# A gated linear recurrence with a spatial gating block on one core: all steps ordered anew, five constant products fewer

## The chip, the core and the metric

The kernel runs on one core of a Trainium2 chip. The metric is the time of one execution on the device, in microseconds. Engines are called by their names: TensorE (PE, with PEld for its weight loads), VectorE (DVE), ScalarE (ACT), GpSimd (POOL) and SyncE (SP, which only starts transfers here).

## The reference, cut to what matters

```
B, H, S, D = 4, 8, 768, 48;  d_model 384, d_ff 1024
# part 1: a recurrence with a complex decay for each of the 4 x 8 heads
a = (a_re, a_im) * min(|a|, 0.999) / (|a| + 1e-6)
for t in range(S):
    S_re, S_im = a_re*S_re - a_im*S_im + k[t] v[t]^T,  a_re*S_im + a_im*S_re
    y[t] = q[t] @ S_re
x = y with the heads side by side                       # (B, S, 384)
# part 2: a block with a gate over positions
h = gelu(x @ w_in);  u, v = halves of h
v_n = layer_norm(v) * g_ln
v_s = w_sg @ v_n + b_sg                                  # mixes the 768 positions
out = x + (u * v_s) @ w_out
```

## The kernel before

**Part 1.** The recurrence is worked in 24 chunks of 128 positions, six to each batch. Thirteen units of one or two chunks prepare them: `load` (steps `l`, `m`), `logs` (`g`: logarithms and exponentials of the gates), `scale` (`e`: the decays multiplied into `k` and `q`), `arctan` (`t`), `turns` (`p`: summed angles), `sincos` (`s`). For each chunk follow `rotate` (`r`), `heads` (`z`: features to rows; for the first batch by TensorE transposes `pk`, later through DRAM), `load_v` (`v`) and `attend` (`a`). `attend` transposes `K` (tile `pk`, copied to `kt`), makes scores `pa` in two halves, masks them into `am`, makes the state's addend `ps` and the output `py`, which takes `am` and the state `S`.

**Part 2.** `normal` (`n`) makes the v half (`pv`), Gelu and the layer norm; `expand` (`x`) makes the u half (`pu`); `spatial` (`y`) mixes positions (`pvs`), multiplies with `u` (`tg`) and makes the output products (`po`). Each operand of these is split into a high and a low part (`xh`, `xl`, `vh`, `vl`, `gh`, `gl`), and each product is made of three. The weights are split in steps `w`; `h` and `k` look at the ranges of the inputs, and `ok` (`in_range`, L858 and after) makes one flag of them which every engine reads before the last branch.

**The order.** Every step is a Python generator; a step is what it issues up to its next `yield`. The string `ORDER` (L32) names the steps one by one: `a8:2` runs two steps of chunk 8's `attend`. Each engine works its instructions in exactly that order. A quote behind a name makes a choice, by the variable `alt`: `ew` (L199) takes VectorE, or GpSimd for one quote; `evac` (L203) takes ScalarE, or VectorE for a quote; `high` (L209) takes ScalarE, GpSimd or VectorE; `low` (L218) VectorE or GpSimd. In `attend`, one quote masks by ScalarE and GpSimd (L656, L657), otherwise VectorE does it in one step (L659). `stoke` (L221) issues no, one or several constant products of 256 columns, by the quotes: they have no use in the result. Two of TensorE's instructions make one such product. `act` (L187) loads another function table whenever a step's function is of another of three sets (Ln and Exp; Arctan and Sin; Gelu).

**Narrow and wide.** Products `pa`, `ps`, `py` and `pd` take weights of at most 64 columns of the array; all others take 96 or 128.

Of the kernel before, what the change touches and what calls it, by code (L numbers as in the profile page):

```python
# [37 lines left out]
a1:2 v2 w7'' w4 w9 w4 a1:2 w12 l4 w2'' t3 s2 r2:2 p2 r3 l4 w12 g3:2 r3 g3:4 w9' w9 a1 p3 w12 m3:2 z2:2 e3 z2:5 w1'' z2
e3 w12 w8 g4:2 e3 v3 p3 e3' w12' e3 a2 a2'' a2 n0_0 a2 g4 w5 a2 w4' a2 g4:2 p3 a2'' a2 v4 a2:2 e3:2 w8'' w8' e3'' e3
e3' e3 n0_0' f z3:3 z3'' p3:2 p3'' p3 f z3:3 f:2 z3 a3:3 f:2 a3 s3:3 w12 e3 a3'' a3:4 n0_0' a3 r4'' r4 w5 w10 t4 p4 v5  # L40
w10:2' w4'' r5'' g4 n0_0:2 z4:6 n0_0:3 z4 r5'' a4 a4'' o0 z4 n0_0:2 g4 l5:2 a4:2 z5:2 w5 a4'' a4 z5' z5:2 m4 z5 g4 m4
z5:2 n0_2 w5 l7 g4 g5 w5 a5 a4:2 a4'' w11 a5' n0_2 a5 a5'' a5' w14 p4:2 e4 n0_0' n0_0'' a4 e4 o1 w11 n0_2'' n0_2 v7
# [1011 lines left out]
```

## Time and profile before

| what | before |
|---|---|
| three runs, us | 437.07, 436.69, 436.38 (median 436.69) |
| span of the profiled execution, us | 434.6 |
| median of the runs less that span, us | 2.1 |
| instructions in the profile | 10107 |
| DMA | 93.54 MB, mean 215 GB/s |

The profile is of one execution. Its span goes from the first to the last instruction; the profile gives no separate time of that execution around the span, so the difference to the median of the runs stands for it. An engine's busy time is the union of its instructions' times; TensorE's products overlap, and their ends are modelled, so that its busy share says less than the distance from one start to the next.

### The profile page before, as it was taken

The numbers are of one execution on the slowest core, as the hardware profiler recorded it, in microseconds if no ns is written. First come the engines' busy times: TensorE is split into PE (matmuls) and PEld (weight loads), VectorE is DVE, ScalarE is ACT, GpSimd is POOL, SyncE is SP. The second block draws the span as 40 slices with busy tenths as digits, with TensorE's granted clock in tenths as the row PEclk, the third lists the DMA queues.
The fourth block names the chain that finished last, engine by engine and source line by source line (L and its number), as shares of the span: only waits on it lengthen the run. The fifth ranks groups of instructions, "written<-read, shape, count | busy, mean of one in ns | idle before, by whom it ended". The sixth has DMA issues, their size and how long they took to land.

```text
span 434.6 us, 10107 instructions
## 1 busy us (share of the span) xinstructions
PE 421.3 (97%) x3958; PEld 383.6 (88%) x3958; DVE 364.5 (84%) x620; ACT 275.2 (63%) x378; POOL 150.7 (35%) x234
## 2 busy tenths in 40 slices
PE   7999899999999989999999999999999999999994
PEld 6667688788999989889998999989999998899994
DVE  5899899999999999898898999997898776757363
ACT  6999898886999886695666776776750113342010
POOL 7214356203334154446022416532321011326130
PEclk9999999999999999999999999999999999999999
DMA  7577868789478898697959789568947964554531
GB/s 244 176 205 196 268 168 278 223 241 277 149 196 259 243 299 263 208 273 212 271 141 299 217 241 252 168 193 226 320 120 230 330 193 163 187 181 166 157 116 59
DMA packets 78540, 93.54 MB, mean 215 GB/s; under 512 B 10516, under 2 KB 60438, under 8 KB 78488
## 3 DMA queue, kind: packets, MB, share of 16 engines
q1 hardware_dynamic: 78344, 92.65, 71.2%
q8 instruction: 32, 0.52, 0.5%
q10 hardware_dynamic: 144, 0.20, 0.1%
q14 instruction: 20, 0.16, 0.1%
HBM read 69.23 MB, written 23.60 MB: 214 GB/s over the span
## 4 chain that ended last, share of the span: by engine, by line
PE 43%; DVE 29%; issue 8%; POOL 7%; ACT 6%; DMA 4%; SPq 0%; DVEq 0%; POOLq 0%
PE pvs L230 10%; PE pu L230 6%; PE po L822 6%; PE pv L230 4%; PE pa L649 4%; PE py L700 2%; PE pv L225 2%; DVE am L659 2%; PE py L705 2%; DVE tg L838 2%; DVE im L510 2%; PE warm L225 2%; ACT L193 1%; PE ps L675 1%; ACT csn L194 1%
## 5 line engine op out<-in xcount | busy, mean ns | idle before, releaser
L230 PE MATMUL pvs<-wsgh,vh 128*128 128x384 f32 x192 | 65.9, 343 | 0.0
L230 PE MATMUL pvs<-wsgh,vl 128*128 128x384 f32 x192 | 65.3, 340 | 0.2
L193 ACT ACT_TABLE_LOAD x50 | 64.2, 1283 | 1.7 <-PEq L1039 0.9
L230 PE MATMUL pvs<-wsgl,vh 128*128 128x384 f32 x192 | 64.9, 338 | 0.0
L649 PE MATMUL pa<-Q,K 96*64 96x64 f32 (+1 forms) x768 | 41.0, 251 | 1.5 <-DVE am L659 1.5
L649 PEld LDWEIGHTS pa<-Q,K 96*64 96x64 f32 x768 | 36.7, 137 | 6.0 <-ACT ep L194 1.6
L700 PE MATMUL py<-am,vbuf 128*64 128x128 f32 x384 | 39.0, 276 | 2.8 <-DVE am L659 1.7
L230 PEld LDWEIGHTS pvs<-wsgh,vl 128*128 128x128 f32 x192 | 36.1, 188 | 1.4 <-DVE vl L219 0.8
L230 PEld LDWEIGHTS pvs<-wsgh,vh 128*128 128x128 f32 x192 | 36.1, 188 | 0.7 <-issue 0.4
L230 PEld LDWEIGHTS pvs<-wsgl,vh 128*128 128x128 f32 x192 | 36.1, 188 | 0.0
L822 PE MATMUL po<-gh,wouth 128*128 128x384 f32 x96 | 33.0, 344 | 0.8 <-DVE oki L873 0.8
L705 PE MATMUL py<-Q,S 96*48 96x128 f32 x320 | 33.7, 272 | 0.0
L822 PE MATMUL po<-gl,wouth 128*128 128x384 f32 x96 | 32.6, 340 | 0.3 <-DVE gl L219 0.2
L230 PE MATMUL pu<-xh,winh 128*128 128x384 f32 x96 | 32.9, 342 | 0.0
L230 PE MATMUL pu<-xh,winl 128*128 128x384 f32 x96 | 32.3, 337 | 0.0
L822 PE MATMUL po<-gh,woutl 128*128 128x384 f32 x96 | 32.3, 337 | 0.0
L230 PE MATMUL pu<-xl,winh 128*128 128x384 f32 x96 | 32.3, 336 | 0.0
L659 DVE TENSOR_TENSOR am<-pa,masks 128x512 f32<-128x512 f32 x44 | 29.5, 682 | 2.4 <-PE pa L649 2.1
L219 POOL TENSOR_TENSOR gl<-tg,gh 128x384 fp32r<-128x384 f32 x15 | 18.6, 1237 | 34.0 <-DVE gh L216 15.1
L700 PEld LDWEIGHTS py<-am,vbuf 128*64 128x64 f32 x384 | 25.5, 136 | 5.2 <-DVE am L659 3.1
L230 PE MATMUL pv<-winh,xh 128*128 128x512 f32 x72 | 29.4, 408 | 0.0
L194 ACT ACTIVATE vr<-pv 128x512 f32<-128x512 f32 x24 | 14.3, 599 | 22.7 <-PE pv L230 13.7
(286 smaller groups left out, 1125.2 us busy)
## 6 DMA issues: line engine op xcount, KB each, us to landing
vbuf<-in_t_v_dram SPq DMA_DIRECT2D x24, 288.0 KB, 3.9
K<-rk SPq DMA_DIRECT2D x18, 384.0 KB, 4.4
Q<-rq SPq DMA_DIRECT2D x18, 384.0 KB, 6.8
x<-xd SPq DMA_DIRECT2D x9, 576.0 KB, 5.6
xd<-yp SPq DMA_DIRECT2D x48, 96.0 KB, 3.5
gr<-in_f_im_dram SPq DMA_DIRECT2D x12, 384.0 KB, 5.3
gr<-in_f_re_dram SPq DMA_DIRECT2D x12, 384.0 KB, 3.9
out_dram<-x SPq DMA_DIRECT2D x23, 192.0 KB, 3.5
```

The costliest lines, as they stand in the source:

```text
L193: nc.scalar.preload_act_table_set(SETS[t])
L194: nc.scalar.activation(out, in_, func, scale=scale, **kw)
L219: ew().tensor_tensor(out=l, in0=src, in1=h.bitcast(F32), op=ALU.subtract)
L225: nc.tensor.matmul(o, mask[:, 0:n], u_turn[:, 0:o.shape[1]], start=True, stop=True, skip_group_check=True)
L230: nc.tensor.matmul(o, w(i), x(i), start=(i == 0 and j == 0), stop=(i == n - 1 and j == 2))
L510: nc.vector.tensor_tensor_scan(out=im[:, kt, :], data0=im[:, kt, :], data1=im[:, kt, :], initial=run["left", b, c0][:, kt:kt + 1] if c0 el ...
L649: nc.tensor.matmul(pa[rows, hh, j:], K(h)[:, j:j + KB], Q(h)[:, j:], start=True, stop=True)
L659: nc.vector.tensor_tensor(out=pairs(am), in0=pairs(pa), in1=causal, op=ALU.mult)
L700: nc.tensor.matmul(py[64 * e:64 * e + 64, p_, :], Vy(h)[:, 0:64], ams[h // 4][:, h % 4, :], start=True, stop=c == 0)
L705: nc.tensor.matmul(py[64 * e:64 * e + D, p_, :], Sb[:, h, :], Q(h), start=False, stop=True)
L822: nc.tensor.matmul(po[d], w[:, f, ds], g[:, f, :], start=f == 0 and j == 0, stop=f == NF - 1 and j == 2)
L838: ew().tensor_mul(tg, us[f], tg)
```

## The change

`ORDER` is replaced: 1179 names become 1457. The same steps are run, each as often; what is new is their order, and the quotes. Counted over both orders, the constant products go from 40 to 35: one ahead of `pl` of chunk 0, one each ahead of a `pk` of chunks 0, 1 and 5, and one ahead of `py` of chunk 5 go. Three generators are written so that a step reads a name later than before, and adds no instruction. The diff, with the order cut to its first and last lines:

```diff
 ORDER = """
-o0:2 l0:2 f' f:10 f' f:10 f:2' g0:5 g0' f:4 f' f:4 f' w0:4 f w0'' f t0 f' f:3 v0 w13 f' w13:3 w13'' f:3 w13' g0:2 m0:2
-f e0' w0 l1:2 g1:2 g1'' f' e0 e0'' f' f:6 f' f:2 e0 w2 p0 p0' p0 w2 s0'' g1:2 g1'' w2 s0:2 e0 w1 t1 r0'' f p0 r0 w1 l2
...
-x0_3 h5 y3_3:2' y3_3:2 y3_0 y3_0'' y3_3:6 h23 y3_0 k4 h3 y3_0' y3_0:2 x3_0 k4 h3 x3_0 y3_0'' x3_0:2 h23 y3_0:2' y3_0:2
-y3_0:2'' y3_0' y3_3 h22:2 x3_0 k5 k7:2 y3_0:2 k5 ok:2 y3_0 x3_0 y3_0:2 y3_0' y3_0'' y3_0:10
+f' f:2 l0 f:2 l0 f:2 g0 f:4 g0:2 f' f:5 g0 f w0 f g0 f:3 f:2' w0 t0 w0 f w0 f l1 f g0 w13 f v0 f' g0 w13 m0 f o0 w13
+f:2 g0 w13 f f' f:2 f' f:3 l1 f' w2 f w0'' f o0 f g1 e0' f f' g1 e0 f' w13' f g1'' e0' e0 f m0 g1 f:2 g1 f:2 f' p0 w1
...
+x3_0 k4 h17 y3_3 y3_0 h1 y3_3 y3_0'' y3_3:2 h3 y3_3 h1' y3_3:2 x3_0 h7 y3_0' y3_0 k10 f x3_0 y3_0:2 k8 x3_0:2 y3_0'
+y3_0 y3_3 y3_0 k12:2 y3_0 k8 y3_0 y3_0' y3_0'' y3_0' y3_0:4 y3_3 y3_0 y3_0' h7'' y3_0:2' y3_0 ok y3_0:7 ok y3_0
 """
@@ logs
-        re, im = (part(n, x) for x in ("re", "im"))
+        re = part(n, "re")
...
+        im = part(n, "im")
         ew().tensor_mul(im, im, e)
@@ scale
-        q_, k_ = (U[n][x] for x in ("q", "k"))
...
-            ew().tensor_mul(at(k_, i), at(k_, i), at(em, i))
+            k_ = at(U[n]["k"], i)
+            ew().tensor_mul(k_, k_, at(em, i))
...
-            ew().tensor_mul(at(q_, i), at(q_, i), at(ep, i))
+            q_ = at(U[n]["q"], i)
+            ew().tensor_mul(q_, q_, at(ep, i))
@@ attend
-        Sb = run.get(("S", g - 1))
+        Sb = lambda: run["S", g - 1]
...
-                nc.vector.tensor_tensor(out=Sn, in0=ps[0:2 * D], in1=Sb, op=ALU.add)
+                nc.vector.tensor_tensor(out=Sn, in0=ps[0:2 * D], in1=Sb(), op=ALU.add)
...
-                    nc.tensor.matmul(py[64 * e:64 * e + D, p_, :], Sb[:, h, :], Q(h),
+                    nc.tensor.matmul(py[64 * e:64 * e + D, p_, :], Sb()[:, h, :], Q(h),
```

## Rows read from the trace of the kernel before

**Rows 1.** The page's first part: busy time of each engine, its share of the span, and its instructions.
```profile
PE 421.3 (97%) x3958; PEld 383.6 (88%) x3958; DVE 364.5 (84%) x620; ACT 275.2 (63%) x378; POOL 150.7 (35%) x234
```
**Rows 2.** The page's fourth part, the chain of work that ended last, by engine.
```profile
PE 43%; DVE 29%; issue 8%; POOL 7%; ACT 6%; DMA 4%; SPq 0%; DVEq 0%; POOLq 0%
```
**Rows 3.** Busy time by stretch. The columns are the stretch, its length, then busy time and instructions of PE, PEld, DVE, ACT and POOL, the granted clock, the DMA share and GB/s.
```profile
20.00:63.30 43.30, 41.38 (x480) 30.50 (x478) 40.28 (x67) 39.74 (x60) 17.48 (x19) 1.00 0.77 220
63.30:155.80 92.50, 91.47 (x941) 84.58 (x940) 89.46 (x139) 80.99 (x108) 30.93 (x53) 1.00 0.78 231
155.80:429.40 273.60, 270.87 (x2486) 255.94 (x2483) 221.40 (x390) 138.94 (x190) 91.60 (x116) 1.00 0.71 212
```
**Rows 4.** The view of waits, TensorE's products alone: what it waited for, us in all, how often, the longest.
```profile
PE py L700 <- DVE am L659: 1.7, 2, 1.3
PE pa L649 <- DVE am L659: 1.5, 1, 1.5
PE py L700 <- POOL am L657: 0.9, 1, 0.9
PE po L822 <- DVE oki L873: 0.8, 1, 0.8
```
**Rows 5.** Constant products (L225) ahead of three tiles: count of instructions (two to a product), shortest, median and longest duration in ns, first and last start in us.
```profile
L225 PE MATMUL pl<-u_turn,masks x8: 379/379/634, 6.4 to 15.4; 128*128 128x256 f32 x8
L225 PE MATMUL pk<-u_turn,masks x6: 379/379/379, 19.0 to 72.6; 128*96 128x256 f32 x6
L225 PE MATMUL py<-u_turn,masks x2: 379/431/483, 77.7 to 78.0; 128*128 128x256 f32 x2
```
**Rows 6.** Instructions in order of time, TensorE and ScalarE, around the first chunk's `pl`: start us, duration us, instruction, and in brackets the idle time before it with what is taken to have ended it.
```profile
6.40 1.03 PE L225 MATMUL pl<-u_turn,masks 128*128 128x256 f32 x2
7.26 0.82 PE L425 MATMUL pl<-re,twice 128*128 128x384 f32 x2
7.92 0.81 PE L426 MATMUL pl<-l,ident 128*128 128x384 f32 x2
...
8.82 0.58 ACT L194 ACTIVATE lo<-pl,cols 128x384 f32<-128x384 f32 x1 [0.91 <-POOL of_head L247]
```
**Rows 7.** The same view, TensorE, at one change from wide to narrow weights and one from narrow to wide.
```profile
166.11 0.34 PE L230 MATMUL pvs<-wsgl,vh 128*128 128x384 f32 x1
166.29 0.34 PE L230 MATMUL pvs<-wsgh,vl 128*128 128x384 f32 x1
166.56 0.56 PE L649 MATMUL pa<-Q,K 96*64 96x128 f32 x8
...
353.78 0.39 PE L700 MATMUL py<-am,vbuf 128*64 128x128 f32 x4
354.00 0.39 PE L705 MATMUL py<-Q,S 96*48 96x128 f32 x4
354.32 0.44 PE L230 MATMUL pvs<-wsgh,vh 128*128 128x384 f32 x1
```
**Rows 8.** The page's fifth part, the table loads: count, then busy us in all and mean ns, then idle time before.
```profile
L193 ACT ACT_TABLE_LOAD x50 | 64.2, 1283 | 1.7 <-PEq L1039 0.9
```
**Rows 9.** Groups of instructions with the same columns: steps that the new order gives to another engine.
```profile
L205 DVE COPY kt<-pk 128x384 f32<-128x384 f32 x19 | 10.2, 547 | 0.4 <-PE pk L631 0.2
L207 ACT COPY kt<-pk 128x384 f32<-128x384 f32 x11 | 5.2, 469 | 1.2 <-PE pk L631 1.2
L585 DVE TENSOR_TENSOR k<-k,csn 128x768 f32<-128x768 f32 x8 | 7.6, 956 | 0.2
L585 POOL TENSOR_TENSOR k<-k,csn 128x768 f32<-128x768 f32 x1 | 1.8, 1849 | 3.1 <-DVE em L585 3.1
L585 POOL TENSOR_TENSOR q<-q,csn 128x768 f32<-128x768 f32 x2 | 4.3, 2160 | 9.7 <-issue 9.7
L219 DVE TENSOR_TENSOR gl<-tg,gh 128x384 fp32r<-128x384 f32 x17 | 9.4, 553 | 4.9 <-POOL gh L214 2.5 <-ACT gh L194 1.6 <-POOL kt L626 0.6
L219 POOL TENSOR_TENSOR gl<-tg,gh 128x384 fp32r<-128x384 f32 x15 | 18.6, 1237 | 34.0 <-DVE gh L216 15.1 <-ACT gh L194 14.5 <-DMA K<-rk 3.0
```
**Rows 10.** Instructions in order of time near the end: the range check's product, the next output product, and the last block's last multiplication.
```profile
423.48 0.19 PE L871 MATMUL pok<-ones,ok 128*1 128x2 f32 x2
424.44 0.41 PE L822 MATMUL po<-gh,wouth 128*128 128x384 f32 x1 [0.77 <-DVE oki L873]
425.29 1.02 POOL L838 TENSOR_TENSOR tg<-u__5361,tg 128x384 f32<-128x384 f32 x1 [4.50 <-DVE tg L835]
```
**Rows 11.** The copy `left` (shortest, median and longest duration in ns over its six instructions), and the instructions around its third one in order of time.
```profile
L522 DVE COPY left<-csn x6: 154/164/2639, 84.2 to 263.0; 128x3 f32<-128x3 f32 x6
...
157.99 1.97 DVE L522 COPY left<-csn 128x3 f32<-128x3 f32 x1
158.11 1.82 POOL L466 TENSOR_TENSOR k<-k,em 128x768 f32<-128x768 f32 x1
160.60 0.44 PE L700 MATMUL py<-am,vbuf 128*64 128x128 f32 x4 [1.33 <-DVE am L659]
```

More of the change, by code (lines that the diff above doesn't have):

```diff
@@ L38 @@
[L38 to L42, printed above, removed]
@@ new lines @@
+w6 p1 e1 z0 w6' s1 m1 g2 a0 g2 a0:2 w6' s1:2 w1 e1'' t2 z0'' z0 g2 l3 g2:2 z0' e1 g2 w2 w3 a0 r1'' p2 r1'' z1 g2 w13
+p2' p2 g2 z1'' w3 z1 e2 z1 p2 e2 w3 g3 o1 e2 f w3 z1:2 f o1 w3'' m2 w3 l3 a0 z1 e0 g3 p2:2 v1 a0 e1 m2 w4 a0 e2' g3 p2
+e2 a1 a1'' w1' a0' s2' z1 a1:2 w1' e2' g3 e2 a1'' g3 f s2 v2 e2' a1:3 w4 g3 w4 o0 s2 w4 t3 g3 p2 l4 r3 g3:2 r2 w7 p3
+z3 e2 r2 f w7 g3 a0 e2 v3 z2 w12 g3 a1' w4'' e3 l4 e3 m3 w7'' z2 r3 z2 w12:2 g4 z3 z2:2 g4 e3 p3 z2 a1 z2 g4' w9 w12
+a2 z2' e2 a2'' m3 p3 a2 w8 e3:2 a2 z3 e3' g4 f e3 w9'' e3' w9 n0_0 z3 f p3:2 z3 e2 e3 z3 p3 w5 a2 w8 z3 w4'' a3 a2 z3
@@ new lines @@
+g4 a2'' p3 s3 w8 e3' n0_0 a2 a3:2 a2' w2' l5 s3:2 w5 t4 a2 a3 a3'' a3:4 n0_0' w5 r4'' g4 n0_0 r4 n0_0 w10 z4 w12 r5''
+e3 v4 p4 n0_0 w5 w10:2 n0_0 z4:2 z5 z4:2 w12' n0_0:2 z4 n0_2 v5 m4 a3 z4 n0_2 z5 z4 a4 e3 a4'' l6 r5' w11 a4 p4 w14 z5
+g5 z5' g4 a4 a4'' l5 z5:2 n0_0 n0_0' a4 z5 a4' z5 n0_2'' g4 a5 g5 a4:2 a5 g4 a5 a5'' p4 w11 a4 m4 f w11'' g5 n0_0 w5
+p4 a5 p4 n0_0 a5 e4 v6 a5 p4 s4' e4 n0_2 e4 e4'' f n0_3 w15 s4:2 g5 t5 g5 w14 e4 f w5 r6:3 n0_0'' r6 r6'' n0_3'' r6
+n0_0 n0_3'' r6'' n0_3'' w15 g6 x0_3 n0_0'' w15:2 n0_2 x0_3 w15' p5:2 n0_2 p5 g5 w15' n0_2 x0_3 f n0_3 w14 g5 x0_3 w14
@@ new lines @@
+x0_3 r6 z6 z7 n0_3:2 x0_0 a7' n0_2 z7 f g5 a6 n0_2 n0_2'' a6 g5 f n0_3 z6 p5 n0_3 w14 w14' a7 a6 n0_3 l7 a6 x0_3:2 a6
+a7 n0_3 p5 a6 f l6 e5 e4 p5 g6 n0_3 s5 n0_3 a7'' e4'' a6:2 x0_0' a6:2 n0_3'' f v7 a6 n0_3' m5 a7 a6 m5 a7'' g6'' a7
+a7'' n0_3'' x0_0'' n0_3:2'' f e5'' e5 a6' a7:2 l7 g6 n0_3' s5 n0_3'' n0_3 a6 s5 n0_3'' a7'' a7 v8 r8 y0_3:2 t6 r8 x0_3
+y0_3 x0_0 r8'' e5 g6 r8 e5 y0_3 y0_3' r8'' g7 r8 y0_3 r8 y0_3 x0_0 g6 z8 y0_3'' y0_3' r8 y0_3' p6 y0_3:2 y0_3'' g6 p6
+z9 l8 g6 z8 y0_3 x0_0:2 a7 p6 y0_3:2 z9 y0_3 x0_0 g6 p6 a9 y0_3 a8 m6 e6 y0_3'' f y0_3 a7 a8 a9:2 p6 m6 g7 s6'' f v9
@@ new lines @@
+y0_3 a8 a8' a8 a8'' y0_3 s6:2 e5 a8 g7' e6'' e5' g7 r10 f a8 e6 l8 a8 r10 r10'' a8 r10 a8' y0_3 a9 g7 a9 f e6'' a8 a9
+f e6 g7 v10 r10'' a9 y0_3:2 r10 t7 a8' g7 z10 a9 y0_3 g7 x0_0 p7 y0_0 r10' g7 g8 y0_0 f p7 y0_0 r10 e7 y0_3 g8 p7 g8
+y0_0 g8 y0_0' y0_0 m7 x0_0 a10:2 a8 y0_3 z10 y0_0 m7 a10 y0_0'' z11 p7 a9 e7 y0_0' g8 p7 a9 g8 e7 g8 a9' p7 a9 a10:2
+l9 a10 s7' t8 y0_3 e7' s7 e6 z11 l9 a10 e6 a10'' a10:2 p8 s7 a10 e7 r12 a10 p8 a11 g8 a9 g9:2 n1_0 a9 a11' v12 v11 r12
+a10 p8 r12'' r12 n1_0 a11 a10 r12 a11'' y0_0' y0_0:2 n1_0 y0_0' r12 m8 y0_0'' y0_0 r12' y0_0 x0_0 e7 a11 z13 n1_0 a11
@@ new lines @@
+y0_0 g8 y0_0 n1_0 r12 p8:2 n1_0 y0_0' n1_0 g9' n1_0 y0_0 n1_0:2 e7 a11 y0_0 e8 p8 s8 z12:2 n1_3 y0_0:2 n1_0 e8'' n1_0
+m8 y0_0 a12 y0_0 a12' a12 n1_0 a13' y0_0 g9 a12' s8 a12 a12'' s8 t9 n1_3'' l10 n1_0 p9 a13 r14 n1_3'' r14 n1_0 g9 z13
+a12 e8 a12'' a12 n1_0'' a13 y0_0 x1_3 g9 n1_0'' x1_3 a13 l10 n1_3 e8'' e8 r14 n1_0' n1_0 n1_3 n1_0 r14 v13 r14'' n1_3
+n1_0:2' n1_3:4 z14 e8 p9 l11 a12 a13 n1_3 a12 n1_3 r14 a13 g10 y0_0 a12' a13 a13'' n1_3 a13 g9 a13 a13'' a13 n1_3' a14
+n1_3 g9 m9 r14 p9 z15 a14'' r14 e8 n1_3:2'' n1_3' g9 g10 y0_0 a14 a12 p9 n1_3'' x1_3 g10 n1_3'' x1_3 n1_3 x1_3 n1_3
@@ new lines @@
+y1_3 x1_3 v14 p9 y1_3 s9'' g10 e9 s9 a14 y1_3' e9'' z14 z15 x1_3 y1_3' s9 x1_0 a13 r16 y1_3' y1_3 v15 a15:2 e9 x1_0
+a15 m9 a14 y1_3 g10 a14:2 a14'' a14 a15 r16 a14 r16' g11 x1_3 e9'' g10 e9 t10 a15 y1_3' a14' g10 a14 y1_3' r16 a13 l11
+a15:2 y1_3 a15 x1_0'' a15 r16' y1_3 z16 x1_0 r16 a14 m10 y1_3 a15 g10 p10:2 v16 a16 y1_3 y1_3' p10 y1_3' x1_0 r16 a16
+l12 g11 p10 a15'' g12 a15 g10 e10 a16 p10 a14 y1_3 r16 g11 z16 y1_0 y1_3 z17 y1_3 s10 g11 y1_3'' y1_3:2 y1_0 y1_3 e10
+a15 p10 h19 s10 a16' s10 t11 y1_3 z17 m10 e10 y1_3:2 h19 y1_3:2 y1_0 r18'' g11 x1_0 p11 v17 a16 y1_3 a16'' e9 g11 a16
@@ new lines @@
+r18 r18' a16'' a16 g11 y1_3 a17 r18 e10 l12 p11 n2_0 a16 e9 a16' a16 y1_0' k2 a17'' e10 a17:2 r18'' p11 g11 a15 r18
+x1_0 g11 r18' m11 z18 f a17 y1_0' p11 x1_0 p11 x1_0 a16 y1_0 p11 y1_0 a16 x1_0 e11 r18 k2 y1_0'' y1_0' y1_0'' y1_0:2
+n2_0 g12 a17'' y1_0 n2_0' y1_0'' h14 y1_0' y1_0 k9 y1_0 n2_0:2 h14 z19 s11' x1_0 n2_0 k9 y1_0' y1_0'' n2_0:2 y1_0 s11
+v18 e11 n2_0:2 s11 g12 m11 a17 v19 y1_0 h13 y1_0 r20' z18 n2_0 a19' a18 a19:2 g12 a19 z19 e11 r20 a18 n2_0 y1_0 r20'
+g12 n2_3 y1_0:2 n2_0 y1_0 e11'' y1_0 a18 a18' a18 n2_0' n2_0 a18 g12 e10 a18 n2_0' n2_0'' r20 e10'' a18:2 n2_0'' e11
@@ new lines @@
+h10 z20 a19 y1_0 a18:2 a19'' a19 n2_3 t12 y1_0 a19 r20'' n2_3' a19:2 n2_0 h10 h18 h13 p12 a19 a18' g12 n2_0'' h18 h6
+a19 n2_3 x2_0 h0 n2_3 h5 p12 n2_3 p12 n2_0 n2_3:2 n2_0' n2_3 r20 n2_3:2 x2_3 n2_3 x2_3:2 a20' v20 a20 h0 r20'' a20
+n2_3 m12 h5' n2_3 h9 n2_3' x2_3 n2_3' r20 a18 z21 v21 h20 p12 n2_3 x2_3 z20 x2_3 n2_3'' h6 n2_3:2'' n2_3 x2_3 n2_3''
+g12 y2_3 x2_0 k0 y2_3 x2_0'' p12 y2_3' s12'' y2_3'' y2_3' h20 y2_3 x2_0 x2_3 s12:2 y2_3 g12 y2_0 x2_0 y2_3 y2_3'' e12
+y2_0 h9 y2_3' a19' e12 y2_3 a21 r22 a20:2 e12 m12 z21 a21 k0 h12 k3 a19 r22 a20 e12' e11 a20 a20' a20 y2_3 x2_0 k7
@@ new lines @@
+y2_3 r22' e11'' y2_3'' y2_3' e12 y2_3 a20 a21 h8 a21 y2_3 r22:2 a21 r22 k3 a20' a20 a21'' y2_3'' a21 k1 a21' a21:2
+y2_3' h8' a21:2 y2_3' a20 v22 z22 h12 z23 r22 h2 x2_0 k1 y2_3 y2_0'' y2_3:2 r22 f y2_3 a20 y2_3 a21' h11 y2_3:2 x2_0
+y2_0:2' z22 y2_0 y2_3 x2_0 y2_0 y2_0' y2_3 x2_0 y2_0' h4 y2_0 z23 y2_0 h2 a21 a22 a22' a22 v23 a22' a22 a22' x2_0 n3_0
+y2_0:2 e12 a22 h11 h15 e12'' a22' a22:3 a23 a22 a23 a22 a23 a22 a23'' y2_0' h15 k6 n3_0' y2_0 h4 h16 a23 f n3_0' y2_0
+a23 n3_0:2 k7 y2_0 a23 y2_0 n3_3 n3_0 y2_0 n3_0:2 y2_0' k5 n3_0:4 y2_0 n3_3'' y2_0 n3_3 n3_0 y2_0 n3_0:2' y2_0 h16
@@ new lines @@
+y2_0:3 n3_3 n3_0' k6 n3_0:2 n3_0' y2_0 n3_0' n3_0'' n3_3:3 n3_0 n3_3:5 k11 n3_3:2 n3_3'' y2_0 n3_3:2 x3_3:2 k4 h22 k11
+x3_3 n3_3' x3_3 x3_0 x3_3 n3_3'' x3_3 n3_3:2' x3_3 n3_3 y3_3:2 y3_3' y3_3'' x3_0' y3_3' k5 h23 y3_3 h21 y3_3 y3_3'
+y3_3 y3_3' x3_3 y3_3 x3_0 y3_3 x3_0 h22 y3_3 h23 y3_3'' x3_0 k10 y3_3 h21 h3 y3_3:2 h17 x3_0 y3_3' y3_3'' y3_0 y3_3'
+x3_0 k4 h17 y3_3 y3_0 h1 y3_3 y3_0'' y3_3:2 h3 y3_3 h1' y3_3:2 x3_0 h7 y3_0' y3_0 k10 f x3_0 y3_0:2 k8 x3_0:2 y3_0'
+y3_0 y3_3 y3_0 k12:2 y3_0 k8 y3_0 y3_0' y3_0'' y3_0' y3_0:4 y3_3 y3_0 y3_0' h7'' y3_0:2' y3_0 ok y3_0:7 ok y3_0
```

40 lines of the change are left out of this document (1 added, 39 removed).

## The prediction

> **What bounds the kernel now.** I read the page's busy times first [rows 1]: TensorE is busy 421.3 of 434.6 us, VectorE 364.5, ScalarE 275.2, GpSimd 150.7. So TensorE alone can set the time, and the only other engine that is near is VectorE. The chain that ended last [rows 2] then shows that the busy share hides something: only 43% of the chain lies on TensorE and 29% on VectorE. The table by stretch [rows 3] says where each of the two holds. I cut it at the output products of chunk 3 (63.3 us) and of chunk 9 (155.8 us). Between them, 92.5 us long, TensorE idles 1.0 us and VectorE 3.0 us; ScalarE has 11.5 us to spare. VectorE and TensorE are both full there. After 155.8 us TensorE idles 2.7 of 273.6 us while VectorE has 52 us free: there TensorE alone decides. The view of waits [rows 4] names what TensorE's idle time is made of: masked score tiles (`am`) that come late from VectorE (1.7 and 1.5 us) or GpSimd (0.9), and 0.8 us at the range check near the end. The granted clock is 1.00 in every stretch [rows 3], so nothing is to be had from it, and since TensorE stays as busy, I take nothing off for it.
>
> I expand both orders into instructions, generator by generator, and compare counts. TensorE's real products are the same ones, and so are the 341 DMA issues. What differs is the five constant products, the engine of steps with a choice, the number of table loads, and the order.
>
> **Constant products, 40 to 35.** The order drops one ahead of `pl` of the first chunk, three ahead of the transposes `pk` (chunks 0, 1, 5) and one ahead of `py` of chunk 5; the 11 on `warm`, three of `pl`, one of `pg` and the 20 of chunk 3's `pv` stay. Each is two instructions [rows 5] of some 0.2 us pitch. They are worth what follows them:
> - `pl`: 6.40 to 7.26 us, 0.86 us [rows 6]. The second real product ends at 8.73 and ScalarE's `lo`, 0.91 us idle before it, starts at 8.82 [rows 6]; the row names a GpSimd step, but what ends at that point is the product. So `lo`, and the table load and `Exp` queued behind it, come about 0.86 us earlier. I take 0.86 us in full (between 0 and 0.9).
> - `pk`: 3 x 0.43 = 1.3 us of TensorE. They lie before 73 us, where TensorE, VectorE and ScalarE are within 2 us of each other in load [rows 3]. Half is gained: 0.65 (0 to 1.3).
> - `py`: it stands in front of a wait on `am` that ends last anyway (the 0.9 us on GpSimd [rows 4]). Nothing is gained.
>
> **Narrow and wide weights.** A wide product ahead of another wide one has a pitch of 0.18 us, ahead of a narrow one 0.27 (166.29 to 166.56): 0.09 more. Four narrow products take 0.22 us ahead of narrow ones and 0.32 ahead of a wide one: 0.10 more [rows 7]. A round trip costs 0.2 us. Counted in both orders, the stretches of narrow products (`pa`, `ps`, `py`, `pd`) fall from 22 to 21 only: 0.2 us. That is the whole of what this part of the change can bring.
>
> **Engines.** VectorE issues 35 instructions fewer. Ten copies `kt` out of PSUM go to ScalarE (10 x 0.547 = 5.5 us off VectorE, 10 x 0.469 = 4.7 on to ScalarE); six rotations (L585) go to GpSimd (5.8 us off, four of 1.85 and two of 2.16 = 11.7 on); of the low halves `gl` four go there (2.2 off, 4.9 on) [rows 9]. The other moves are of the same kind and smaller; with the mean of each step's rows the sums are VectorE -21 us, GpSimd +29 us and 22 instructions, ScalarE +3.6 us. And ScalarE's steps change between Ln/Exp, trigonometry and Gelu 64 times, not 50: 14 more table loads of 1.283 us [rows 8], +18 us. So the new order buys VectorE time with GpSimd and ScalarE time, neither of which is the bound over the whole span.
>
> But stretch by stretch it is less. Sums of the steps that stand ahead of chunk 9's `py` in the order: VectorE's work up to there is the same (+0.4 us), because what was saved before chunk 3 (-2.6 us) is spent behind it. In the full stretch of 92.5 us VectorE's work goes from 88.3 to 91.3 us, and ScalarE's from 80.8 to 88.5, five table loads among it. The 21 us on VectorE fall nearly all after 155.8 us, where VectorE is not the bound. What is left is that late `am` tiles become rarer: the rows price the three kinds at 4.1 us [rows 4], and the new order takes VectorE's weight splits and copies out of the way in some of these places and not in others. I take half, -2.1 us (0 to -4.1). ScalarE's 7.7 us in the full stretch have 11.5 us of idle time as their cover [rows 3]; the idle time is made of waits, so not all of it is cover. I take +0.7 us (0 to +7.7).
>
> **The end.** Before, the range check stands ahead of 27 products of the last block: TensorE's `pok` starts at 423.48 and the next product at 424.44 [rows 10], because every engine reads the flag there. In the new order the read comes behind all TensorE work, and ahead of the last store alone, whose data take six more products and an addition. What remains of 0.96 us is about 0.2 for `pok` itself: -0.75 us. Of the last quarter of that block the multiplication stays on GpSimd (1.02 us [rows 10]) and both halves go there too, from VectorE (1.2 us for the low one [rows 9], less for the high one); the cover is 27 products x 0.174 = 4.7 us against a chain of about 3.9, the first step on VectorE counted. If that cover were short, it costs up to 0.5 us.
>
> **Edits in the generators.** Reading `im`, `q`, `k` and the state later only lets a step stand earlier in the order; no instruction is added, so they cost nothing. Of the moved DMA issues, the first chunks' `re` go ahead of `im` and the gates' check loads move; all are on SyncE's queue, which computes nothing, and the first two loads stay first.
>
> **Sum.** -0.86 - 0.65 - 0.2 - 2.1 + 0.7 - 0.75 = -3.86 us. The profiled span of 434.6 becomes 430.7. The median of the runs shown, 436.69, lies 2.1 us above that span; with the same 2.1 us around it the time is 432.8 us. A measurement of this kernel tells some 0.2%, 0.9 us, from no change.
>
> **Rivals.**
> (a) *ScalarE takes over in the full stretch (slower).* If its waits there stay 11.5 us and its work is 88.5, the stretch takes 100 us and not 92.5: +7.5, less 2.5 us of the sure gains, gives about 441.7. It decides from the point at which ScalarE's idle time can't shrink below some 8 us. For it: 64 loads, and 96% of the stretch. Against it: part of ScalarE's work that stands ahead in the order is not needed until later, and the loads are not on the chain by name. 0.15.
> (b) *Nothing reaches TensorE but the ends.* VectorE remains full to 155.8 us, and the order trades one late `am` for another: only `pl` and the end count, 435.1 to 436.7. 0.14.
> (c) *Most waits go.* All `am` waits, all `pk` products, and waits shorter than the view lists: -7.5 or more, 427 to 429.5. 0.12. For it: VectorE has 16 us more room by the end.
> (d) *GpSimd blocks VectorE.* The copy `left` of three columns takes 0.16 us by median and 2.64 at most; at 157.99 us it lasts 1.97, while a GpSimd product of 1.82 us runs, and TensorE's next `py` waits 1.33 us for the `am` behind it [rows 11]. Two of the six copies were held, and this one reached TensorE. If GpSimd's 29 us each met a busy VectorE (84% of the time [rows 1]) and held it, VectorE would lose 24.7 us for 21 gained: +3.5 us, less 1.8 from the ends, 438.4. Against it: in the full stretch GpSimd's work stays at 31 us by the order, and later VectorE has room. 0.04.
> The Trainium skill states the rule of (d) in "SBUF — State Buffer", section "Who interferes with whom": the second port pair is held by VectorE or GpSimd for a whole instruction and the other blocks fully, two-input VectorE instructions included where GpSimd reads. By that rule (d) would be the likely case; the trace agrees for single instructions (2.64 us against 0.16), not for the sum.
>
> **Numbers.** The forecast itself has 0.55 (429.5 to 435). Faster by over 0.2%: 0.55 + 0.12 + part of (b), 0.72. Within 0.2%: 0.10. Slower: (a) without its mildest outcomes, (d), and mishaps at the end, 0.18. The range reaches down into (c), 427.5, and up through (d) and the lower half of (a), 439.5.
>
> **What would show it.** Right: the first `lo` near 8.0 us; no product of L225 into `pk` or `py`; `pok` followed within 0.3 us; TensorE's waits on `am` under 2.5 us in sum; VectorE near 344 us, ScalarE near 297, GpSimd near 180; 64 table loads. Wrong: chunk 9's `py` later than 156 us, ScalarE at 95% up to there with TensorE waiting on `kt` or score copies from it (a), or VectorE's total not falling (d).

## The result, and the profile after

| what | before | after |
|---|---|---|
| median of the four runs, us | 436.88 | 440.79 |
| ratio, with its 95% interval | | 1.0108 (1.0072 to 1.0143) |
| profiled execution: time, span, us | -, 434.6 | 441.16, 439.3 |
| py of chunk 3, of chunk 9, last `po`, us | 63.3, 155.8, 429.4 | 65.9, 161.0, 433.9 |

The kernel is slower by 1.1%, not faster by 0.9%. The two profiled spans differ by 4.7 us: +2.6 up to `py` of chunk 3, +2.6 from there to chunk 9's, -0.7 to the last output product, +0.2 behind it. The loss is over by 161 us; the rest of the order even gains a little. Each trace is of one execution, and not always a middle one: after's took 441.16 us for a median of 440.79, that of e1 below 437.18 for 439.50, that of z1 437.32 for 434.83. Three traces with the order of before up to chunk 9 (before, y2 and z1 below) reach it at 155.8, 156.7 and 157.5 us, so that a difference of 1 to 2 us between two traces says little.

The page after, busy times and the chain by engine (lines of before: [rows 1], [rows 2]):
```profile
PE 421.4 (96%) x3948; PEld 382.8 (87%) x3948; DVE 364.3 (83%) x586; ACT 293.5 (67%) x405; POOL 184.7 (42%) x256
...
PE 48%; DVE 7%; ACT 5%; POOL 3%; issue 2%; DMA 1%; DVEq 0%; POOLq 0%; ACTq 0%
```
VectorE issues 34 instructions fewer and is as busy as before. ScalarE (+18.3 us) and GpSimd (+34.0) got about what the counts promised (+21.6 and +29). The chain on VectorE fell from 29% to 7%, which on its own would have been read as relief.

The page after, table loads (L193 is now L199), against [rows 8]:
```profile
L199 ACT ACT_TABLE_LOAD x64 | 82.1, 1283 | 2.0 <-PEq L1047 0.9
```
Busy time by stretch after, cut at the same products as [rows 3]; columns as there:
```profile
20.00:65.90 45.90, 41.78 (x481) 30.80 (x478) 43.69 (x66) 42.67 (x65) 21.26 (x25) 1.00 0.78 229
65.90:161.00 95.10, 92.81 (x942) 85.39 (x941) 92.13 (x142) 86.34 (x112) 33.12 (x47) 1.00 0.77 225
161.00:433.90 272.90, 269.30 (x2480) 254.76 (x2475) 217.02 (x357) 149.19 (x206) 118.90 (x136) 1.00 0.71 209
```
Length less PE's busy time is TensorE's idle time: 4.1, 2.3 and 3.6 us, before 1.9, 1.0 and 2.7. In the second stretch VectorE is at 97% in both kernels, and ScalarE has 8.8 us to spare. Idle time makes 1.3 of the 2.6 us by which that stretch is longer; most of the rest lies in short pauses that overlapping products hide. From one start to the next, pauses of over 0.15 us beyond the usual distance of two such products add up to some 1.4 us there before (0.9 of it on the `am` of GpSimd) and to 3.7 after: 1.3 on `am` in four places, 0.8 on `Q`, 0.6 on `vl`, 0.4 each on `q` and on a u tile, 0.2 others.

The view of waits after, TensorE's products alone (columns as [rows 4]):
```profile
PE py L708 <- DVE am L667: 3.1, 5, 1.1
...
PE pa L657 <- ACT xh L200: 1.8, 1, 1.8
PE pu L236 <- DVE xl L225: 1.4, 2, 0.9
PE pa L657 <- ACT Q L213: 0.7, 1, 0.7
PE py L708 <- POOL am L665: 0.6, 2, 0.3
PE pa L657 <- DVE am L667: 0.6, 2, 0.3
```
Before, the rows for `am` add up to 4.1 us. Now they are 4.3, and the 1.8 put down to `xh` is one more late `am`, as the next view shows: 6.1. Waits for `xl`, `Q` and `vl`, of which the view before names none, come on top. The row `po <- oki` is gone. The same view for the stretch from 65.9 to 161 us alone, where before has the one row on `am` of GpSimd (0.9):
```profile
PE pa L657 <- ACT Q L213: 0.7, 1, 0.7
PE pvs L236 <- POOL vl L225: 0.5, 1, 0.5
PE pa L657 <- DVE am L667: 0.3, 1, 0.3
PE pk L609 <- POOL q L582: 0.3, 1, 0.3
PE py L708 <- DVE am L667: 0.3, 1, 0.3
```

The instructions around chunk 3 after, in order of time:
```profile
58.81 1.05 DVE L699 TENSOR_TENSOR S<-S,dec 96x384 f32<-96x384 f32 x1 [1.00 <-DMA dec<-row]
...
59.79 0.54 DVE L549 SCALAR_TENSOR_TENSOR csn<-csn,phi 128x384 f32<-128x384 f32 x1
60.25 0.94 DVE L225 TENSOR_TENSOR wsgl<-raw,wsgh 128x768 fp32r<-128x768 f32 x1
...
61.12 0.68 DVE L667 TENSOR_TENSOR am<-pa,masks 128x512 f32<-128x512 f32 x1
61.95 0.89 PE L657 MATMUL pa<-Q,K 96*64 96x128 f32 x16 [1.79 <-ACT xh L200]
62.02 1.82 POOL L225 TENSOR_TENSOR xl<-x,xh 128x768 fp32r<-128x768 f32 x1 [2.57 <-ACT xh L200]
62.32 1.86 DVE L279 TENSOR_SCALAR bits<-raw 128x512 int32<-128x512 int32 x1
...
64.11 0.67 DVE L667 TENSOR_TENSOR am<-pa,masks 128x512 f32<-128x512 f32 x1
64.83 0.44 PE L708 MATMUL py<-am,vbuf 128*64 128x128 f32 x4 [1.11 <-DVE am L667]
```
The scores of the first half, 16 products from 56.59 us on, were complete at 57.5, but their `am` stands on VectorE behind a state product that waits 1.00 us for a DMA, a phase step and a weight part: it runs at 61.12, and the second half of the scores, which takes the same PSUM buffer, idles for 1.79. The next `am` stands behind `bits`, a step of 0.42 us that lasts 1.86 beside GpSimd's `xl`; `py` idles for 1.11. Not all of this comes from the order of these steps: e1 below begins with the same 341 steps, and in its trace the DMA is waited for 0.36 us, `bits` lasts 1.35, and `py` of chunk 3 is done at 63.8 and not at 65.9.

I also summed, over VectorE's instructions, what each lasts beyond the lower quartile of its own kind and shape. It is 19.1 us before (38 of 42 such instructions run beside a GpSimd one) and 38.4 after (55 of 56). The undisturbed work, summed instruction by instruction, falls by 17 to 20 us, by the length that is taken as undisturbed; 21 were predicted. GpSimd's hold takes it back.

### The profile page after: what moved, and what is told of

Its sections match the earlier page's. It is cut to its first block, busy times and chain, and to the rows that moved or that the text cites. A ratio compares the mean times of both kernels' runs of the same rounds, so it can differ in the third digit from the quotient of the medians.

```text
span 439.3 us, 10115 instructions
## 1 busy us (share of the span) xinstructions
PE 421.4 (96%) x3948; PEld 382.8 (87%) x3948; DVE 364.3 (83%) x586; ACT 293.5 (67%) x405; POOL 184.7 (42%) x256
## 4 chain that ended last, share of the span: by engine, by line
PE 48%; DVE 7%; ACT 5%; POOL 3%; issue 2%; DMA 1%; DVEq 0%; POOLq 0%; ACTq 0%
PE pvs L236 17%; PE po L830 10%; PE pu L236 8%; PE pv L236 7%; PE pa L657 2%; PE py L708 2%; PE py L713 2%; POOL am L665 1%; ACT L199 1%; PE pk L639 1%; DMA im<-in_u_im_dram 1%; ACT csn L200 1%; ACT vr L200 1%; DVE xl L225 1%; DVE bst L777 1%
## 5 line engine op out<-in xcount | busy, mean ns | idle before, releaser
L657 PE MATMUL pa<-Q,K 96*64 96x128 f32 (+1 forms) x768 | 42.8, 251 | 3.3 <-ACT xh L200 1.8
L225 POOL TENSOR_TENSOR gl<-tg,gh 128x384 fp32r<-128x384 f32 x19 | 25.1, 1323 | 27.0 <-ACT gh L200 18.4
L713 PE MATMUL py<-Q,S 96*48 96x128 f32 x320 | 32.8, 272 | 0.0
L200 ACT ACTIVATE vr<-pv 128x512 f32<-128x512 f32 x24 | 14.3, 598 | 24.5 <-PE pv L236 18.3
L708 PEld LDWEIGHTS py<-am,vbuf 128*64 128x64 f32 x384 | 24.1, 136 | 7.4 <-DVE am L667 5.4
```

The lines of the kernel that those rows point to most:

```text
L200: nc.scalar.activation(out, in_, func, scale=scale, **kw)
L225: ew().tensor_tensor(out=l, in0=src, in1=h.bitcast(F32), op=ALU.subtract)
L657: nc.tensor.matmul(pa[rows, hh, j:], K(h)[:, j:j + KB], Q(h)[:, j:], start=True, stop=True)
L713: nc.tensor.matmul(py[64 * e:64 * e + D, p_, :], Sb()[:, h, :], Q(h), start=False, stop=True)
```

## The experiments

Orders are named by their steps, 1605 in each. `ORDER` of before and after differ in place and in the choice of engine.

**Which part of the order.** New order up to `py` of chunk 3 (341 steps), the rest in the order of before; and the reverse.
```diff
-(order of after)
+e1: first 341 steps of after, then before's remaining steps
+e2: first 344 steps of before, then after's remaining steps
```


> The new order up to the output products of chunk 3, then the old order's remaining steps. In the two traces chunk 3's py ends 2.6 us later with the change, and 1.5 us less work of TensorE lies ahead of it. Theory 'early': those 2.6 us are lost there by operands that come late and stay lost; then 439.5 us against 436.9 of before. Theory 'ScalarE' (table loads in the full stretch behind chunk 3 are the cause): nothing of it is in this kernel, 436 to 437.

> The old order up to the output products of chunk 3, then the new order's remaining steps. 'Early': 436.9 + (4.6 - 2.6) = 438.9 at most, about 438. 'ScalarE': all of the loss, 440 to 441.

e1: 439.50 us, 1.0058 (1.0036 to 1.0081). e2: 442.60, 1.0130 (1.0102 to 1.0158). The time between `py` of chunk 3 and of chunk 9, in the view by stretch (columns as [rows 3]), in e1 and then in e2:
```profile
63.80:157.10 93.30, 91.54 (x939) 84.35 (x939) 89.78 (x137) 80.28 (x107) 30.15 (x47) 1.00 0.75 219
```
```profile
64.50:162.50 98.00, 93.55 (x941) 85.14 (x941) 94.23 (x144) 86.45 (x112) 30.40 (x46) 1.00 0.79 229
```
With the old order the stretch takes 92.5 us (before) or 93.3 (e1), with the new one 95.1 (after) or 98.0 (e2). So the start alone is not the cause: e2, with the old start, is no better than after. e1 lies where 'early' put it, e2 3.7 us above what 'early' allowed. By the medians the new start costs 2.7 us and the new rest 5.8, while both together cost 3.9: the parts don't add up.

**Order and engines apart.** The steps of one order with the engine choices of the other; 206 of 1605 choices change, constant products stay with the order.
```diff
-w13'' ... e0'' ... s1'       (before: engines of before)
+w13'  ... e0'  ... s1        (e3: order of before, engines of after; e4: the reverse)
```


> The old order with the new order's choice of engine for every step (40 constant products kept, 50 table loads). If the engines are the cause (VectorE blocked by 22 more GpSimd instructions, or copies queued on ScalarE): 439 to 441. If the order is: 436 to 438, a little slower since the choices were made for another order.

> The new order with the old choice of engine for every step (35 constant products, 64 table loads). If the order or the table loads are the cause: 440 or more. If the engines are: 437.

e3: 492.01 us, 1.1287 (1.1248 to 1.1325). e4: 479.55, 1.0994 (1.0954 to 1.1033). Waits of TensorE in e3:
```profile
PE pv L230 <- POOL xl L219: 9.3, 1, 9.3
PE py L702 <- DVE am L661: 8.1, 5, 2.5
```
But for ScalarE's 14 table loads, e3 has the counts of after on VectorE, ScalarE and GpSimd, and it loses 55 us: counts by engine alone do not tell the time. Neither choice of engines fits the other order.

**GpSimd's hold on VectorE.** In both orders every full-width GpSimd step with an SBUF input becomes one column of it and fills.
```diff
-        return nc.gpsimd if alt[0] == 1 else nc.vector
+        return fills if alt[0] == 1 else nc.vector
+    # fills: the operation on column 0, then two memsets of the whole output (one for `high`)
```


> The kernel before, in which every step that its order gives GpSimd with an SBUF input of full width is replaced by the same operation on one column and fills (memsets) of the whole output, which take about as long and read nothing; those steps' results are not what they should be. Theory 'GpSimd holds VectorE': VectorE loses about 19 us of busy time and the time falls by 1 to 3 us (TensorE's late waits shrink). Rival 'the waits come from the order alone': VectorE stays near 364 us and the time within 1 us.

> The kernel after with the same replacement. Theory 'GpSimd holds VectorE': VectorE falls by about 38 us (to some 325), the time falls by more than in the kernel before, and the difference between the two orders, 3.9 us, shrinks to 1 or less or turns round. Rival 'the order alone, or ScalarE': VectorE may fall, but the difference between the two stays at 3 to 5 us.

433.15 us, 0.9911 (0.9885 to 0.9937), and 436.40 us, 1.0002 (0.9985 to 1.0019). Busy times with fills, first in the order of before, then of after:
```profile
PE 420.3 (97%) x3958; PEld 383.6 (89%) x3958; DVE 347.7 (80%) x620; ACT 275.3 (64%) x378; POOL 147.5 (34%) x384
```
```profile
PE 419.5 (96%) x3948; PEld 382.8 (88%) x3948; DVE 329.4 (76%) x586; ACT 293.5 (67%) x405; POOL 181.3 (42%) x451
```
GpSimd is as busy, VectorE loses 16.8 and 34.9 us, and what its instructions last too long falls to 1 us in each. So the hold is real and costs 3.5 and 4.4 us of time. But it was there before; of the 3.9 us between the orders it makes 0.7, and by the intervals above this may be some 2 us more or less. The difference stays within the rival's 3 to 5 us. In the traces the stretch between the two `py` takes 92.5 us with fills in the order of before and 94.1 in that of after, for 92.5 and 95.1 without: 1.0 of its 2.6 us may be the hold, as far as two traces can tell.

**Table loads.**
```diff
+        if table_of.get(func, 0):
+            func, bias, kw = AF.Copy, None, {}
```


> The kernel before with ScalarE's arctan, sine and Gelu turned into copies, so that no table load is left but the first; those results are not what they should be. 50 loads (64 us of ScalarE) become 1. Theory 'ScalarE's loads cost the time': the time falls by 2 us or more. Theory 'GpSimd holds VectorE': it falls by under 2 us.

> The kernel after with the same edit: 64 loads (82 us of ScalarE) become 1. Theory 'ScalarE's 14 added loads cost the time': the difference between the two orders, 3.9 us, shrinks to 1 or less. Theory 'GpSimd holds VectorE': it stays at 3 us or more.

440.33 us, 1.0071 (1.0045 to 1.0097), and 442.10, 1.0111 (1.0081 to 1.0141). Some 65 and 84 us less of ScalarE make neither kernel faster. The difference shrinks to 1.8 because the order of before loses 3.7: ScalarE's steps come elsewhere, `pk` waits 1.8 us for a DMA at 191 us and a stretch at half the clock follows. (The trace of the order of after has such a stretch too, at 292 us.) 1.8 lies between the two theories: that the loads cost the 4 us is out; a part of them can't be excluded by this.

**Single late steps.** Ten steps of after moved a few places, chosen from its ten largest waits. In the diff below, cut at the dots, `S691(a2)` is a state product of chunk 2, `csn(p3)` a phase step, `wsgl(w8)` and `bits(w5)` are weight parts.
```diff
-... a2'' S691(a2) csn(p3) wsgl(w8) am(a3) ... bits(w5) pa am(a3) ...
+... a2'' am(a3) S691(a2) csn(p3) wsgl(w8) ... pa am(a3) bits(w5) ...
```


> The kernel after with ten of its 1605 steps moved a few places and nothing else: five `am` steps (a0, a2, a3, a6, a8) ahead of weight parts and others that stand before them on VectorE, three steps put behind what TensorE waits for (the bits of w5 and the `left` copy of p7 behind the `am` of a3 and a10, ScalarE's vr of n0_0 behind the copy of Q of chunk 5), two `xl` steps (n1_3, x1_0) one place earlier. They are the steps named by ten waits of TensorE in the trace of after that add up to some 8 us. Theory 'a few late steps on VectorE's queue make the loss': 433.5 to 437.5, the stage to chunk 3 some 3 us shorter than in after. Rival 'VectorE's queue as a whole is late, each wait that is removed comes back at the next product': over 438.5.

443.65 us, 1.0165 (1.0142 to 1.0187). `left` of p7 now stands behind the sine's first step too and reads changed phases. `py` of chunk 3 came at 62.9, 3.0 us earlier as expected, and by chunk 8 nothing of it was left: `pvs` waits 1.4 us for `vl` at 117 us, and the granted clock falls (the view by stretch, as all such rows below; the clock stands ahead of the DMA share):
```profile
121.00:125.00 4.00, 4.00 (x16) 4.00 (x15) 3.93 (x7) 3.94 (x5) 0.00 (x0) 0.57 0.62 192
```
The rival holds. z3 keeps only the moves up to chunk 3, with that `vl` on VectorE; z4 has the same start with the order of before behind it, and the two moves of z1.
```diff
+z3: am of a0, a2, a3 earlier; bits(w5) behind am(a3); vl(n0_3) on VectorE
+z4: z3's first 341 steps, then z1's
```


> The order of after with five of the ten moves, those up to chunk 3 (the `am` of a0, a2 and a3 earlier, the bits of w5 behind the second `am` of a3), and the last vl of n0_3 on VectorE and not on GpSimd, for which TensorE waited at 117 us once it came earlier. Theory 'two late steps at chunk 3 make the early loss': py a3 at some 63 (65.9 in after) and the time 2 to 3 us below after, 437.5 to 438.8. Rival 'it comes back at the next product': 440 or more.

> The order of after up to py of chunk 3 with the same early moves, then the order of before with the two moves of z1. e1_new_to_c3 (the same start unrepaired, then before) was 2.5 us slower than before. Theory 'the start loses only by its two late steps, and the two moves of z1 hold': 434 to 435.5. Rival 'it comes back': 437 or more.

z3: 441.68 us, 1.0107 (1.0080 to 1.0135). z4: 436.63, 0.9992 (0.9973 to 1.0011). In z3 `py` of chunk 3 is at 62.7, as expected, and of chunk 9 at 160.8, where after has 161.0:
```profile
62.70:160.80 98.10, 93.43 (x940) 85.23 (x941) 94.89 (x146) 88.44 (x115) 32.00 (x49) 1.00 0.76 223
```
Its four largest waits in that stretch, 3.6 of 4.5 us (0.7 of the rest are on `am`):
```profile
PE pk L609 <- DVE k L582: 1.0, 1, 1.0
PE pvs L236 <- DVE vl L225: 1.0, 1, 1.0
PE pk L609 <- POOL q L582: 0.9, 1, 0.9
PE pa L657 <- ACT Q L213: 0.7, 1, 0.7
```
z4 reaches chunk 9 at 157.3, e1 with the unrepaired start at 157.1. In the traces a start that is 1.0 us or 3.2 us faster brings nothing behind chunk 8. For z3 'it comes back' holds by the time too. z4 lies between its two theories: its median is 2.9 us below e1's, the two moves of z1 are worth 1.7 by themselves (below), so that some 1.2 us of the repaired start may stay.

**VectorE's amount of work.** By the sum that sized these runs, VectorE's undisturbed work between the two `py` is 93.6 us in before and 97.3 in after, 3.7 more; with other lengths taken as undisturbed it is 3.0 to 3.2 more, and the busy times above give 2.7. z2 gives before 3.6 us more, w1 takes about 4 out of after, w2 out of z3.
```diff
-        ew().tensor_tensor(out=l, ...)
+        for _ in range(2 if step[0] in (356, 429, 448, 465) else 1):      # z2
+            ew().tensor_tensor(out=l, ...)
-            ew().tensor_mul(k_, k_, at(em, i))
+            ew().tensor_mul(cut(k_), cut(k_), cut(at(em, i)))   # w1, w2: five steps on 1/8 of the columns
```


> The order of before, only four low-part subtractions of VectorE between py a3 and py a9 (w4, w11, n0_3, w5: 0.66 + 0.94 + 1.36 + 0.68 = 3.6 us) are done twice, which changes no result. In after VectorE has 3.7 us more undisturbed work in this stretch than in before (97.3 for 93.6) and TensorE takes 2.6 us longer for it. Theory 'VectorE, 97% busy there, bounds the stretch': py a9 comes 2 to 4 us later and the time rises by 2 to 4 us. Rival 'single late steps of the new order make the loss, the amount of work doesn't': under 1 us.

> The order of after, only that five in-place products of VectorE between py a3 and py a9 (im of g5, k and q of e4, k and q of e5; 0.95 us each) work on an eighth of their columns, so that the rest keeps its old values; about 4 us less for VectorE in the stretch. Theory 'VectorE's amount of work up to py a9 sets the time of py a9': it comes 2 to 4 us earlier than in after (161.0) and the time is 437 to 439. Rival 'single late steps': under 1 us earlier, 440 or more.

> z3_after_early_moves with the same five products cut to an eighth. z3 brought py a3 3.2 us earlier and lost it all again by py a8. Theory 'VectorE's amount of work': now part of it is kept, py a9 at 156 to 158.5, 435 to 438. Rival: as w1_after_less_vector or z3, 440 or more.

z2: 440.38 us, 1.0071 (1.0044 to 1.0098). w1: 441.37, 1.0092 (1.0059 to 1.0125). w2: 440.44, 1.0084 (1.0066 to 1.0101). z2's 3.6 us cost 3.9; `pu` waits 2.1 us for a weight part, then the clock falls, which costs 1.7 of it:
```profile
100.00:104.00 4.00, 4.00 (x17) 3.90 (x17) 3.33 (x7) 0.94 (x3) 2.17 (x7) 0.57 0.85 270
```
w1's median is not better than after's, against the theory; three of its seven runs, 438.4 to 439.1 us, lie where the theory put them, the other four at 441.4 and more. In its profiled execution (443.09) the waits at chunk 3, of the same size as in after, go with 6.9 us at half the clock, from 62.3 to 69.2. This part of it lies behind chunk 3's `py`:
```profile
65.90:69.20 3.30, 3.30 (x8) 2.63 (x9) 3.30 (x5) 1.87 (x2) 0.00 (x0) 0.51 0.52 166
```
It costs 1.6 us (3.3 x 0.49); without it the stretch to chunk 9, 96.6 us, would take 95.0, for 95.1 in after: nothing gained. w2, where the clock stays, reaches chunk 9 at 159.5, z3 at 160.8, and the medians differ by as much, 440.44 and 441.68 in tight runs. So 4 us of VectorE's work are worth some 1.2 us in w2 and nothing that can be seen in w1: too little for the theory.

**The products and the end.** y3 takes only the five constant products out of before; y2 has the end of after.
```diff
-g0' z0' z1' z5' a5'     (one quoted step of each; a quote is a constant product)
+g0  z0  z1  z5  a5      (y3)
+y2: before up to n3_3's first product, then after's remaining steps
+y4: y3, the end of y2, and the am of a1, a2, a5, a10 earlier (w12, w1 and left(p7) behind them)
```


> The order of before, only with the five constant products taken out that the change takes out (one ahead of pl of g0, three ahead of pk in z0, z1 and z5, one ahead of py of a5): 35 and not 40. The prediction's terms: 1.5 us faster (0.86 + 0.65 + 0), 435.2. Rival 'the products filled idle time': within 0.4 us of before.

> The order of before up to the first product of n3_3 (374.7 us), from there on the order of after. Theory 'the new end gains for itself, about 2 us (the stall at pok of 0.6 and small ones)': 434.5 to 435.5 at a before of 436.7. Rival 'the end's gain only gives back what the waits ahead of it left behind': 436.2 or more.

> The order of before with all of it: the five products out, the end of after from n3_3 on, and its three largest waits taken away by moves (parts of w12 and w1 behind the `am` of a1 and a2, the `left` copy of p7 behind the `am` of a10, the first `am` of a5 on VectorE alone). Theory 'a few late steps make the waits': the moves give 2.5 to 4.5 us over the new end and the products, 430 to 433. Rival 'waits come back at the next product': 434 or more.

y3: 436.50 us, 1.0010 (0.9994 to 1.0025): nothing. Its stretches, with the cuts of [rows 3]:
```profile
20.00:63.50 43.50, 41.23 (x479) 30.34 (x477) 40.69 (x67) 40.12 (x60) 16.87 (x19) 1.00 0.76 217
63.50:155.80 92.30, 90.38 (x933) 83.77 (x935) 89.35 (x138) 80.88 (x107) 30.83 (x53) 1.00 0.77 229
```
TensorE's busy time is 1.2 us shorter in the two, and its idle time 1.2 longer. y2: 445.88 us, 1.0208 (1.0187 to 1.0230); y4: 447.11, 1.0235 (1.0209 to 1.0261). Both fail where the two orders are joined: `pu` waits 7.8 us (7.3) for a Gelu tile at 379 us, and half the clock sets in before the wait is over. They tell nothing of the end. In y4 one move is legible all the same: with `left` behind the `am` of chunk 10 its delay against before goes from 2.9 us at chunk 9 to 1.3 at chunk 10.

**Two moves alone.** That move, and the range check as late as in after, in the order of before.
```diff
-... am(a10) left(p7) am(a10) dec(e6) ... ok:2 y3_0 x3_0 y3_0:2 y3_0' y3_0'' y3_0:10
+... am(a10) am(a10) left(p7) dec(e6) ... y3_0 x3_0 y3_0:2 y3_0' y3_0'' y3_0:2 ok y3_0:7 ok y3_0
```


> The order of before with two moves and nothing else: the `left` copy of p7 (1.97 us beside GpSimd) behind the second `am` of a10, for which TensorE waits 1.33 at 159 us, and the final check (13 VectorE steps and `pok`, 0.6 of wait) as far from the end as in after. Theory 'a wait that is removed late in the order, where VectorE has room, stays removed': 1.2 to 2.1 us faster than before. Rival 'each wait comes back at the next product': within 0.6 us of before.

434.83 us, 0.9956 (0.9934 to 0.9979): 0.4% faster than before and faster than after, with 40 constant products and 50 table loads. After and z1 around `left`, VectorE:
```profile
161.54 2.56 DVE L530 COPY left<-csn 128x3 f32<-128x3 f32 x1
162.27 1.80 POOL L478 TENSOR_TENSOR q<-q,ep 128x768 f32<-128x768 f32 x1
...
164.02 0.68 DVE L667 TENSOR_TENSOR am<-pa,masks 128x512 f32<-128x512 f32 x1
```
```profile
160.36 1.39 DVE L524 COPY left<-csn 128x3 f32<-128x3 f32 x1
```
`left` is still held in z1, but both `am` of chunk 10 stand ahead of it (159.16 to 160.44 us), and nothing that TensorE waits for stands behind it.

## Why the prediction was wrong

- **Late `am` waits, -2.1: the step that failed.** It halved the four waits without naming one step that the new order takes out of their way. One went (the 0.9 behind GpSimd), but the same order of work puts other steps in the way: the `am` rows went from 4.1 to 6.1 us, and waits for `xl`, `Q`, `vl` and `q` that were not there came on top. The `left` collision of [rows 11], which I had read, stands in after too and waits 1.07 us.
- **`pl` -0.86 and `pk` -0.65: wrong, 0 measured (y3).** I put a product's length on the path because the step behind it had idled. At `pl` TensorE's pace took most of it in y3 and more than all of it in after. Here is TensorE in y3 and in after, against [rows 6]:
```profile
6.39 1.45 PE L426 MATMUL pl<-re,twice 128*128 128x384 f32 x2
7.67 0.82 PE L427 MATMUL pl<-l,ident 128*128 128x384 f32 x2
```
```profile
6.39 1.49 PE L432 MATMUL pl<-re,twice 128*128 128x384 f32 x2
7.67 1.46 PE L433 MATMUL pl<-l,ident 128*128 128x384 f32 x2
```
  The real products start 0.87 us earlier, but now two or four of them are 0.64 us apart and not 0.33, so that `lo` starts at 8.59 and 9.23, for 8.82 before. It is the pace that all products have up to there: the two constant products of [rows 6] are 0.43 us apart, later ones 0.22. It looks like the lower of the clock's two levels, though the granted clock reads 1.00 there. What is left is lost at the next wait. `py` at 0 was right.
- **VectorE and ScalarE by stretch: right in the main, and not drawn to its end.** VectorE's work up to chunk 9 was to be the same and 3 us more in the full stretch; it is the same to within 0.5 us, and some 3 us more. ScalarE there was to be 88.5, it is 86.3. I priced ScalarE's share (+0.7) and nothing for VectorE's, the engine with 3.0 us to spare. That share is worth nothing to be seen in w1, some 1.2 us in w2 and 2.2 in z2 (3.9 less the clock's 1.7). The full stretch, for which the sum has +0.7, took 2.6 us more.
- **GpSimd (rival d).** Its mark came true: VectorE's total did not fall. The chance of 0.04 was too low for the mark, and the price of 3.5 us was a size for the hold as a whole (3.5 before, 4.4 after), not for the difference of the orders, 0.7 (give or take some 2). The rule of the Trainium skill, "SBUF — State Buffer", section "Who interferes with whom", that a VectorE instruction with two inputs from SBUF contends with a GpSimd instruction that reads SBUF and not with one that only writes it, agrees with x1: instructions of VectorE that lasted 38.4 us too long last 0.9 too long once GpSimd reads almost nothing.
- **ScalarE taking over (rival a): no.** It is at 91% in the stretch, and without the loads nothing was faster. The wait on `Q`, which ScalarE copies, is 0.7 us with the loads and without. "Not on the chain by name" was misread, and changed a chance alone; the page before has, by line:
```profile
PE pvs L230 10%; PE pu L230 6%; PE po L822 6%; PE pv L230 4%; PE pa L649 4%; PE py L700 2%; PE pv L225 2%; DVE am L659 2%; PE py L705 2%; DVE tg L838 2%; DVE im L510 2%; PE warm L225 2%; ACT L193 1%; PE ps L675 1%; ACT csn L194 1%
```
- **The end, -0.75: right.** `pok` at 432.44 is followed by the next product at 432.56, with 0.96 between them before. The span from chunk 9 on is 0.5 us shorter, and z1, with the same move and one more, gains 1.7. **Narrow and wide:** 21 runs as counted; 0.2 us can't be told apart.
```profile
432.44 0.19 PE L879 MATMUL pok<-ones,ok 128*1 128x2 f32 x2
432.56 0.45 PE L830 MATMUL po<-gh,wouth 128*128 128x384 f32 x1
```

Of the signs that were named, the one of being wrong came first: `py` of chunk 9 at 161.0 us, later than 156. The counts of loads, ScalarE's and GpSimd's totals and `pok` came as named; `lo` near 8.0, `am` waits under 2.5 us and VectorE near 344 us did not.

The main place of the loss is shown: from `py` of chunk 3 on the new order reaches chunk 9 some 3.5 to 5.5 us later than the old one from any start (after against e1 3.9, z3 against z4 3.5, e2 against before 6.7 less the 1.2 by which it is late at chunk 3); old-order traces reach it at 155.8 to 157.5 us, new-order ones without a fall of the clock (after, e2, z3) at 160.8 to 162.5. The start costs too, 2.7 us by e1's median. What stands in the stretch is shown as well: after, e2 and z3 all wait there for `Q` from ScalarE (0.7 in each), for `vl` (0.5, 0.5, 1.0), for `q` from GpSimd (0.3, 0.3, 0.9) and for `am` (0.6 to 0.7), while before, y2 and z1 wait for the one `am` from GpSimd (0.9 to 1.1). In the view of e2 for its stretch the rows on `Q`, `vl` and `q` stand as in that of after, and its longest is:
```profile
PE pk L609 <- ACT K L213: 1.5, 1, 1.5
```
The cause behind these waits is settled in part only. VectorE's added work is at most some 1.2 us of it (w2; w1 shows nothing), GpSimd's hold 1.0 by one trace; which of the order's choices makes each tile late stays open. Moving one of them only showed the next.

## What to carry to other kernels

In a stretch where two engines are above 95%, neither a removed product nor a removed wait is a gain until the wait behind it is named. Sums of an engine's work did not tell the time either: 4 us less of VectorE gave 0 to 1.2. Price a new order by the tiles that it makes late, one by one, and take first what is late in the order or has slack behind it. An order and its choice of engines are one thing: either half of this change alone cost 43 to 55 us. Here two moves read from two waits (1.7 us gained) beat a whole new order that takes work off VectorE.
